# Six one-by-one releases of the q, k and v loads in a slot of selective attention, and fewer loads at the start

## The chip, the cores and the metric

One core of a Trainium2 chip runs the whole program. The metric is the device time of one execution in microseconds; the median of several executions counts, and less is better. The engines named below are PE (matmuls; its weight loads are listed as PEld), ACT (exponentials and copies), DVE (vector work), POOL (masks and indirect DMAs) and SP (which issues most DMAs). Each engine takes its instructions in the order in which the program gives them, and engines wait for each other through semaphores.

## The reference

The kernel computes a causal attention with a decaying bias for 8 batches of 8 heads, 576 tokens and head size 64, and then a mixture of eight experts over the tokens, in float32. Cut to what is computed:

```python
scores = scale * np.matmul(q, k.transpose(0, 1, 3, 2))
cum = np.cumsum(np.maximum(s, 0.0), axis=-1)
bias = -(cum[:, :, :, None] - cum[:, :, None, :])
scores = np.where(causal, -1000000000.0, scores + np.minimum(bias, 0.0))
attn = np.exp(scores - np.max(scores, axis=-1, keepdims=True))
attn = attn / (np.sum(attn, axis=-1, keepdims=True) + 1e-09)
x = np.matmul(attn, v)             # then (B,H,S,D) -> (B, S, H*D)
...
logits = x @ w_gate
local_gate = sigmoid(x @ w_local)
# token by token: keep the previous token's expert where local_gate >= 0.5, else argmax(logits)
h = np.maximum(x[b, s] @ w1[e], 0.0)
out[b, s] = softmax(logits[b, s])[e] * (h @ w2[e])
```

## The kernel before

The attention works on 32 pairs of heads (`NPAIR`), pair n being batch n // 4 and two neighbouring heads, which lie on the lower and upper 64 partitions. The main loop (L1002) runs over 16 slots m of two pairs each, 2m and 2m + 1. The program order is that of the Python code; no scheduler moves anything.

A slot has these parts, in this order:

- Scores (`scores`, L893): for each of the two pairs, four units u = 0 to 3 (`UNITS`). A unit is a handful of matmuls of keys by queries into one tile of the pool `ps_s` (three buffers of two PSUM banks), one exponential on ACT into the tile `e{u}` in SBUF (L905), and one or two causal masks on POOL (L890). A slot so has eight units and eight exponentials; `e` tiles have two buffers, one for each pair.
- The places 0 and 1, one after each pair's scores (`at`, L1016): planned work of the router, from slot 4 on. A product (`lp`) or a ranking (`pos`) takes one more `ps_s` buffer at place 1 of every second slot; from slot 6 on POOL stores tokens into a DRAM table with indirect DMAs (scatters, L349), up to five in a slot.
- Values (`values`, L924): for each pair, 200 matmuls a slot in all, in two pieces (query blocks 0 to 5, then 6 to 8), each into `po` in PSUM. Each piece is read out by DVE, a reciprocal into `recs` (L941) and a product (L942).
- Places 3, 4 and 5, and between them weighing (`weigh`, L876): v of a later pair, times the key weights, into one of four `vg` tiles; ACT writes one column (L881), DVE the rest (L884). `WEIGHED` says which pairs are weighed at the end of which slot: 2 and 3 in slot 0, 4 to 7 in slot 1, 8 and 9 in slot 2, and so on.

The inputs come through SP's DMA queue: q and k of a pair 288 KB each into `p_in` (four buffers each for q and k), v of a pair 320 KB into `p_v` (six buffers, `NVA`). At the start q, k of pairs 0 to 3 and v of pairs 0 to 5 are issued without a wait. Later loads are held back so that they do not start at once: before the DMA, ACT copies one element of something that is only ready at the wanted time into the tile to be loaded ("behind"), and the DMA has to wait for that copy. In every slot

- after unit 1 of the second pair, `load_v` of pair 2m + 6 is held behind that unit's exponential (L1014), and v of pair 2m + 7 follows at once, without a copy of its own;
- after the second value piece of the first pair is in `po`, and before DVE reads it out, `load_qk(n + NV)` holds k of pair 2m + 4 behind an element of `po` in PSUM (L1021), and q of that pair and k and q of pair 2m + 5 follow at once.

So a slot has two bursts, one of two transfers of v and one of four of k and q. After the attention the experts run: PE multiplies gathered tokens by w1 and w2 of each expert until the end.

Of the kernel before, what the change touches and what calls it, by code (L numbers as in the profile page):

```python
# [9 lines left out]
F32 = mybir.dt.float32  # L10
# [7 lines left out]
P = 128  # L18
B, H, S, DH = 8, 8, 576, 64
# [3 lines left out]
HP = H // 2  # L23
NPAIR = B * HP
# [11 lines left out]
NJ = S // DH  # L36
NJA = 6
# [8 lines left out]
NV = 4  # L46
NVA = 6
# [2 lines left out]
          ((5, 5), (0, 0, 1, 1, 3, 4, 5, 5)))  # L50
BX = 3
FIRST = ((0, P, 0, 3 * P), (P, S, 3 * P, S))
CAP = N + DH
ROWS = E * CAP + 2 * P
EMPTY = 1 << 20
# [60 lines left out]
class Router:  # L116
# [8 lines left out]
    def constants(self):  # L125
# [8 lines left out]
        self.base0 = self.t("base0", [P, E])  # L134
        nc.gpsimd.tensor_scalar(self.base0, self.eidx, float(CAP), 0.0, Alu.mult, Alu.add)
        self.base = self.t("base", [P, E])
# [18 lines left out]
    def constants2(self):  # L155
# [31 lines left out]
        for i in range(2 * DOUBLE // P):  # L187
            r = 2 * E * CAP + i * P
            nc.sync.dma_start(self.halves[r : r + P], self.pad)
# [190 lines left out]
    def assign(self, name, n, start, k, size):  # L380
# [11 lines left out]
        step = self.s(name + "step", [P, E])  # L392
        v.tensor_scalar(step, n, -float(size), float(CAP), Alu.mult, Alu.add)
        if start is not None:
# [6 lines left out]
        if start is not None:  # L401
            v.tensor_scalar(of[:, 1], r, start[:, 0:1], float(E * CAP), Alu.add, Alu.min)
        else:
            v.tensor_scalar(of[:, 1], r, float(E * CAP), None, Alu.min)
        used = self.s(name + "used", [P, E])
# [72 lines left out]
class Experts:  # L478
# [47 lines left out]
    def load(self, l, layer=None, part=None, behind=None):  # L526

        if l not in self.owner:
            return
        u = self.owner[l]  # L530
        if not part:
            self.e = self.piece(u, self.units[u][2].index(l), 0)
        parts = 1 if part is None else 4
        for i, src in enumerate((self.w1, self.w2)):
            if layer is not None and layer != i:
                continue
            ws = self.ws.setdefault(l, [None, None])
            if not part:
                pool = getattr(self, self.place(l))
                ws[i] = pool.tile([P, FK, D] if i else [P, DK, F], F32, name=f"w{i + 1}b")  # L540
                if behind is not None:
                    self.nc.scalar.copy(ws[i][0:1, 0, 0:1], behind)
            n = ws[i].shape[1] // parts
            c = slice((part or 0) * n, (part or 0) * n + n)
            self.nc.sync.dma_start(ws[i][:, c].rearrange("p c f -> p (c f)"),
                                   src[bass.ds(self.e, 1), :, c].rearrange("o p c f -> (o p) (c f)"))
# [219 lines left out]
def attention(ctx, tc, q, k, v, s, wx, ident, recs, wend, router, experts):  # L766
    nc = tc.nc
# [3 lines left out]
    def pool(name, bufs, **kw):  # L771
        return ctx.enter_context(tc.tile_pool(name=name, bufs=bufs, **kw))

    once = pool("once", 1)
    p_in = pool("p_in", 4)
# [11 lines left out]
    ins, vs, es, xs, xts = {}, {}, {}, {}, {}  # L787
    heads = [slice(DH * h, DH * h + DH) for h in range(2)]

    def load_qk(n, behind=None):  # L790

        if n >= NPAIR:
            return
        b, hp = divmod(n, HP)
        ins[n] = qb, kb = p_in.tile([P, S], F32, name="qb"), p_in.tile([P, S], F32, name="kb")
        if behind is not None:
            nc.scalar.copy(kb[0:1, 0:1], behind)
        for k0, k1, q0, q1 in FIRST if n == 0 else ((0, S, 0, S),):
            nc.sync.dma_start(kb[:, k0:k1], k[b][:, hp, k0:k1])  # L799
            nc.sync.dma_start(qb[:, q0:q1], q[b][:, hp, q0:q1])  # L800

    def load_v(n, behind=None):
        if n >= NPAIR:
            return
        b, hp = divmod(n, HP)
        va = vs[n] = p_v.tile([P, NB, 2, DH], F32, name="va")
        if behind is not None:
            nc.scalar.copy(va[0:1, 0, 0, 0:1], behind)
        nc.sync.dma_start(va.rearrange("p c h d -> p (c h d)"), v[b, hp].rearrange("p c h d -> p (c h d)"))
# [14 lines left out]
    load_qk(2)  # L824
    load_v(2)
    load_qk(3)
    for n in range(3, NVA):
        load_v(n)
    router.projection(wx)
    wk = once.tile([P, NPAIR, G1 + NB, 2], F32, name="wk")  # L830
    nc.gpsimd.memset(wk[:TL, :, G1 + NF], 0.0)
# [18 lines left out]
    def key_exps():  # L850
        nc.scalar.activation(w1, cum[:, : G1 * P], Act.Exp, bias=ref[:, 0:1])
        nc.scalar.activation(w2, cum, Act.Exp, bias=ref[:, 1:2])
# [40 lines left out]
    def scores(n, u):  # L893
        if n >= NPAIR:
            return
        qb, kb = ins[n]
        if u == 0:
            es[n] = [p_e.tile([P, 2, w], F32, name=f"e{i}") for i, w in enumerate(WIDTH)]
        e = es[n][u]
        ps = banks("ps")[:, :, : WIDTH[u]]  # L900
        for c, a, z, at in UNITS[u]:
            key = min(c * P, S - P)
            for h, d in enumerate(heads):
                mm(ps[:, h, at : at + z - a], lhsT=kb[d, key : key + P], rhs=qb[d, a:z], start=True, stop=True)  # L904
        nc.scalar.activation(e, ps, Act.Exp, scale=scale)  # L905
        for c, a, z, at in UNITS[u]:
            m = min(P, z - a)
            if a < c * P + P:
                masked(e[:, :, at : at + m], [[0, 2], [1, m]], P - m)

    def weights_of(n, c, j, h):
        for u, unit in enumerate(UNITS):
            for c1, a, z, at in unit:
                if c1 == c and a <= j * DH < z:
                    return es[n][u][:, h, at + j * DH - a : at + j * DH - a + DH]

    def x_tile(b):

        if b == 2:
            return p_x0.tile([P, NJ, 2, XW], F32, name="xb0")  # L920
        w = experts.w_first.tile([P, FK, D] if b else [P, DK, F], F32, name=f"w{b + 1}b")
        return w.rearrange("p c f -> p (c f)")[:, : NJ * 2 * XW].rearrange("p (j g f) -> p j g f", j=NJ, g=2)

    def values(n, j0, j1):  # L924
        b, hp = divmod(n, HP)
        if b not in xs:
            xs[b] = x_tile(b) if b < BX else p_x.tile([P, NJ, 2, XW], F32, name="xb")
        xb = xs[b]
        po = ps_o.tile([P, j1 - j0, VW], F32, name=f"po{j0}")
        for j in range(j0, j1):  # L930
            last = j // 2 if j < NJ - 1 else NF
            for c in range(last + 1):
                for h, d in enumerate(heads):
                    mm(po[d, j - j0, :], lhsT=weights_of(n, c, j, h),  # L934
                       rhs=vgs[n % NV][:, c if j < 2 * G1 else G1 + c, h, :],
                       start=(c == 0), stop=(c == last))

        def evacuate():
            m = j1 - j0
            rec = recs[:, n, j0:j1, :]  # L940
            nc.vector.reciprocal(rec, po[:, :, VW - 2 : VW])  # L941
            nc.vector.tensor_tensor(xb[:, j0:j1, :, 32 * hp : 32 * hp + 32], po[:, :, :DH].rearrange("p j (g i) -> p j g i", g=2),  # L942
                                    rec[:, :, 0].unsqueeze(2).unsqueeze(3).to_broadcast([P, m, 2, 32]), op=Alu.mult)

        return evacuate, po[0:1, 0, 0:1]

    def turn(n):

# [6 lines left out]
    def turns(pair):  # L955
        for n in pair:
            turn(n)
# [9 lines left out]
    for g in range(NG - 1):  # L967
        m = HP * GB // 2 * (g + 1)
# [9 lines left out]
        for c in range(NC):  # L978
# [3 lines left out]
            i, p = places[c]  # L982
# [3 lines left out]
    m = NPAIR // 2  # L986
# [11 lines left out]
    def at(slot, place):  # L998
        for f in todo.pop((slot, place), ()):
            f()  # L1000

    for m in range(NPAIR // 2):  # L1002
        pair = 2 * m, 2 * m + 1
        for n in pair:
            for u in range(len(UNITS)):
                if (n, u) == (0, 2):
                    key_exps()
                scores(n, u)
                if (n, u) == (0, 3):
                    key_weights()  # L1010
                    weigh(0)
                    weigh(1)
                if (n % 2, u) == (1, 1):
                    load_v(n - 1 + NVA, es[n][u][0:1, 0, 0:1])  # L1014
                    load_v(n + NVA)
            at(m, n - 2 * m)  # L1016
        for n in pair:
            values(n, 0, NJA)[0]()
            evacuate, done = values(n, NJA, NJ)
            if n % 2 == 0:  # L1020
                load_qk(n + NV, done)  # L1021
                load_qk(n + 1 + NV)
            evacuate()
            at(m, 3 + n - 2 * m)
        last = m % HP == HP - 1
        if last:
            turns(pair)
        for n in range(WEIGHED[m - 1] + 1 if m else 2, WEIGHED[m] + 1):
            weigh(n)
        if not last:  # L1030
            turns(pair)
        at(m, 5)
# [575 lines left out]
```

## Time and profile before

| | us |
|---|---|
| median of 3 runs | 729.42 (729.3 to 730.54) |
| the profiled execution | 748.85 |
| its span, first to last instruction | 747.1 |
| first score matmul | 4.84 |
| first expert matmul, after the attention | 221.6 |
| PE, 768 score matmuls (L904), busy | 94.7 |
| PE, 3200 value matmuls (L934), busy | 105.2 |
| ACT, 128 exponentials (L905), busy | 97.0 |
| POOL, 160 masks (L890), busy | 67.2 |

The profile is of one execution with the profiler on; its span is some 18 us above the median of the runs without it.[...] An entry such as "PEld ps <- ACT e" says that a weight load for the score tile `ps` stood still until ACT was done with `e`, which is read from semaphores. "issue" is time in which an engine stood still and nothing that the profile shows held it.

The start of the chain, and the loads as SP issues them (start, length, engine and line, tile):

```profile
0.81 0.39 SPq L799 DMA_DIRECT2D kb<-in_k_dram  x1
...
8.88 1.93 SPq L809 DMA_DIRECT2D va<-in_v_dram  x3
11.20 0.33 SPq L194 DMA_DIRECT2D wx<-in_wx_dram  x1
12.76 0.89 SPq L809 DMA_DIRECT2D va<-in_v_dram  x2
16.13 0.33 SPq L799 DMA_DIRECT2D kb<-in_k_dram  x1
16.51 0.45 SPq L800 DMA_DIRECT2D qb<-in_q_dram  x1
17.05 0.38 SPq L799 DMA_DIRECT2D kb<-in_k_dram  x1
17.48 0.42 SPq L800 DMA_DIRECT2D qb<-in_q_dram  x1
```

The three v at 8.88 are the last of the start, the two at 12.76 are the held ones of slot 0, and the four from 16.13 on are its held k and q.

### The profile page before, as it was taken

Reading aid. Unit: us, or ns where it says so; the run is one execution under the profiler, and the core shown is the slowest. Engines: PE = TensorE matmul, PEld = TensorE weight load, DVE = VectorE, ACT = ScalarE, POOL = GpSimd, SP = SyncE. Lnnn points to the kernel's source line nnn. Section 1 sums busy time; section 2 is a strip of 40 time slices with the busy share of each in tenths; the row PEclk is TensorE's granted clock in tenths of the full one; section 3 lists DMA queues with packets and bytes.
Section 4 is the critical chain, followed back from the end, with each engine's and each line's share of the span. In section 5 each row is a group of like instructions: output and inputs, shape, how many; then the busy total and the mean of one; then the engine's idle time right before and its main releaser. Section 6 shows DMA issues by size and latency. Waiting matters only on the chain.

```text
span 747.1 us, 16231 instructions
## 1 busy us (share of the span) xinstructions
PE 729.2 (98%) x6537; PEld 504.9 (68%) x6537; DVE 257.7 (34%) x714; ACT 166.0 (22%) x355; POOL 206.7 (28%) x453
## 2 busy tenths in 40 slices
PE   8999999999998999999999999999999999999996
PEld 7888878878876567567567365637644676673675
DVE  4656668677756383101100411041132001104110
ACT  4645454354331011011011010201010111110111
POOL 3543367577574245350100011010101001000100
PEclk9999999999998999999999999999999999999999
DMA  8464455665629996598555979996999965976700
GB/s 303 145 189 149 152 191 165 201 199 172 188 81 382 341 396 218 208 424 240 203 190 169 375 258 396 342 382 237 425 334 390 423 215 214 307 268 239 269 15 32
DMA packets 57205, 187.28 MB, mean 251 GB/s; under 512 B 11837, under 2 KB 32061, under 8 KB 49568
## 3 DMA queue, kind: packets, MB, share of 16 engines
q1 hardware_dynamic: 50224, 165.91, 62.3%
q0 software_dynamic: 6800, 20.09, 7.0%
q8 instruction: 53, 0.87, 0.5%
q14 instruction: 32, 0.26, 0.1%
q10 hardware_dynamic: 96, 0.15, 0.1%
HBM read 165.50 MB, written 20.75 MB: 249 GB/s over the span
## 4 chain that ended last, share of the span: by engine, by line
PE 95%; issue 2%; POOL 1%; DVE 1%; DMA 1%; ACT 0%; SPq 0%; POOLq 0%; ACTq 0%
PE yp L637 34%; PE hp L608 31%; PE po L934 13%; PE ps L904 11%; PE hp L599 4%; PE lp L217 2%; DMA qb<-in_q_dram 1%; POOL table L349 0%; ACT e L905 0%; PE pos L301 0%; POOL e L890 0%; PE pos L302 0%; DVE xb L942 0%; SPq L799 0%; POOL out_dram L641 0%
## 5 line engine op out<-in xcount | busy, mean ns | idle before, releaser
L637 PE MATMUL yp<-w2b,hT 128*128 128x512 f32 (+4 forms) x768 | 258.4, 584 | 0.0
L608 PE MATMUL hp<-xT,w1b 128*128 128x256 f32 (+2 forms) x1216 | 232.0, 352 | 0.0
L608 PEld LDWEIGHTS hp<-xT,w1b 128*128 128x128 f32 x1216 | 207.7, 192 | 30.0 <-issue 7.8
L637 PEld LDWEIGHTS yp<-w2b,hT 128*128 128x128 f32 (+3 forms) x768 | 109.9, 167 | 138.4 <-issue 136.1
L641 POOL DMA_INDIRECT out_dram<-y,gi x37 | 36.4, 984 | 412.3 <-DVE y L639 380.0
L610 ACT ACTIVATE hT<-hp 128x256 f32<-128x256 f32 (+2 forms) x152 | 53.6, 353 | 430.4 <-PE hp L608 417.2
L639 DVE TENSOR_SCALAR y<-yp,gi 128x512 f32<-128x512 f32 (+2 forms) x38 | 27.8, 731 | 299.8 <-PE yp L637 293.4
L934 PE MATMUL po<-vg,e 128*64 128x66 f32 x3200 | 105.2, 223 | 6.9 <-issue 5.6
L934 PEld LDWEIGHTS po<-vg,e 128*64 128x64 f32 x3200 | 98.7, 138 | 13.1 <-issue 10.5
L905 ACT ACTIVATE e<-ps 128x768 f32<-128x768 f32 (+1 forms) x128 | 97.0, 837 | 46.5 <-PE ps L904 45.8
L904 PE MATMUL ps<-qb,kb 64*128 64x192 f32 (+4 forms) x768 | 94.7, 398 | 0.6 <-ACT e L905 0.3
L904 PEld LDWEIGHTS ps<-qb,kb 64*128 64x128 f32 x768 | 64.7, 186 | 29.6 <-ACT e L905 14.9
L890 POOL TENSOR_SCALAR_AFFINE_SELECT e<-e 128x256 f32<-128x256 f32 (+1 forms) x160 | 67.2, 444 | 50.3 <-ACT e L905 49.3
L349 POOL DMA_INDIRECT table<-xb,idx x54 | 54.5, 1009 | 19.6 <-issue 16.8
L619 DVE STREAM_TRANSPOSE hT<-hs 32x256 f32<-32x256 f32 x64 | 27.9, 436 | 78.9 <-ACT hs L601 78.1
L884 DVE TENSOR_TENSOR vg<-va,wk 128x256 f32<-128x256 f32 x64 | 41.5, 714 | 0.0
L941 DVE RECIPROCAL recs<-po 128x12 f32<-128x12 f32 x64 | 13.5, 211 | 64.0 <-PE po L934 45.2
L599 PE MATMUL hp<-w1b,xT 128*32 128x512 f32 (+1 forms) x224 | 28.3, 594 | 0.0
L578 DVE STREAM_TRANSPOSE xT<-xq 128x1024 f32<-128x1024 f32 (+1 forms) x23 | 23.6, 1028 | 11.8 <-DMA xq<-table 11.7
L942 DVE TENSOR_TENSOR xb<-po,recs 128x384 f32<-128x384 f32 (+1 forms) x48 | 22.0, 458 | 2.2 <-POOL xb L325 0.6
L599 PEld LDWEIGHTS hp<-w1b,xT 128*32 128x32 f32 (+1 forms) x224 | 8.1, 114 | 17.8 <-issue 17.8
L953 DVE STREAM_TRANSPOSE xt<-xb 128x576 f32<-128x576 f32 x24 | 17.1, 751 | 0.0
(254 smaller groups left out, 202.6 us busy)
## 6 DMA issues: line engine op xcount, KB each, us to landing
w2b<-in_w_dram SPq DMA_DIRECT2D x30, 2048.0 KB
w1b<-in_w_dram SPq DMA_DIRECT2D x29, 2048.0 KB
va<-in_v_dram SPq DMA_DIRECT2D x32, 320.0 KB
kb<-in_k_dram SPq DMA_DIRECT2D x31, 288.0 KB
qb<-in_q_dram SPq DMA_DIRECT2D x31, 288.0 KB
xq<-table SPq DMA_DIRECT2D x56, 130.0 KB
w1b<-in_w_dram SPq DMA_DIRECT2D x4, 512.0 KB
xq<-table SPq DMA_DIRECT2D x20, 65.0 KB
```

The lines of the kernel that those rows point to most:

```text
L349: put = self.nc.gpsimd.indirect_dma_start(out=self.halves, in_=src, element_offset=0, in_offset=None, out_offset=bass.IndirectOffsetOnAxis ...
L599: mm(ps[d, :], lhsT=xT[:, k, d], rhs=self.ws[l][0][:, k, c * 512 : c * 512 + 512], start=(k == 0), stop=(k == DK - 1))
L608: mm(ps[:, :w], lhsT=self.ws[ls[0]][0][:, k, c * P : c * P + P], rhs=xT[:, k, :w], start=(k == 0), stop=(k == DK - 1))
L610: nc.scalar.activation(self.hT[u][:, c, :w], ps[:, :w], Act.Relu)
L619: self.nc.vector.transpose(hT[32 * a : 32 * a + 32, :, 32 * r : 32 * r + 32], hs[32 * r : 32 * r + 32].rearrange("p (c i) -> p c i", i=P)[ ...
L637: mm(ps[d, :], lhsT=hT[:, k, n * P + d.start : n * P + d.stop], rhs=self.ws[l][1][:, k, f : f + w], start=(k == 0), stop=(k == FK - 1))
L641: put = nc.gpsimd.indirect_dma_start(out=self.out[:, :], out_offset=bass.IndirectOffsetOnAxis(ap=gi.bitcast(I32)[:m, n, 0:1], axis=0), in_ ...
L884: nc.vector.tensor_tensor(vg[:, to].rearrange("p c h e -> p (c h) e")[:, :, :DH], va[:, :c].rearrange("p c h e -> p (c h) e"), wk[:, n, to ...
L890: nc.gpsimd.affine_select(out=ap, in_=ap, compare_op=Alu.is_ge, fill=0.0, base=base, pattern=n, channel_multiplier=-1)
L904: mm(ps[:, h, at : at + z - a], lhsT=kb[d, key : key + P], rhs=qb[d, a:z], start=True, stop=True)
L905: nc.scalar.activation(e, ps, Act.Exp, scale=scale)
L934: mm(po[d, j - j0, :], lhsT=weights_of(n, c, j, h), rhs=vgs[n % NV][:, c if j < 2 * G1 else G1 + c, h, :], start=(c == 0), stop=(c == last))
```

## The change

Every load after the start is held by a copy of its own. `parts_of(m)` lists what slot m has to load: v of pairs 2m + 4 and 2m + 5 (in slot 0 none, in slot 1 v of pairs 4 to 7), then k and q of pair 2m + 4 and k and q of pair 2m + 5. `let_go(place, behind)` is called after each score unit (place `e{u}{n % 2}`: unit u of the first or second pair) and after each read-out value piece (place `x{i}{n % 2}`), and where the place is among the slot's points it issues the next part behind that element: an element of the unit's `e` tile, in a column that POOL does not mask, or of `recs`, which DVE writes. In slots 2 to 13 the points are e00 and e20 (v), e01 (k), e21 (q), x00 (k) and x10 (q); slots 14 and 15 have nothing to load. At the start v of pairs 4 and 5 is no longer loaded, and slot 0 no longer loads v of pairs 6 and 7. The k copy no longer reads `po`.

```diff
+POINTS = {0: ("x00", "x10", "x01", "x11"), 1: ("e00", "e10", "e20", "e30", "e01", "e21", "x00", "x10"),
+          2: ("e00", "e20", "e01", "e21", "x00", "x10")}
...
-    for n in range(3, NVA):
-        load_v(n)
+    load_v(3)
...
-        return evacuate, po[0:1, 0, 0:1]
+        return evacuate
...
+    def qk_part(n, what):
+        def load(behind):
+            b, hp = divmod(n, HP)
+            to = p_in.tile([P, S], F32, name=what + "b")
+            ins.setdefault(n, [None, None])["qk".index(what)] = to
+            nc.scalar.copy(to[0:1, 0:1], behind)
+            nc.sync.dma_start(to, (q, k)["qk".index(what)][b][:, hp])
+        return load
+
+    def v_part(n):
+        return lambda behind: load_v(n, behind)
+
+    def parts_of(m):
+
+        v_of = {0: (), 1: range(NV, NV + 4)}.get(m, range(2 * m + NV, 2 * m + NV + 2))
+        return [v_part(n) for n in v_of if n < NPAIR] + [
+            qk_part(n, x) for n in (2 * m + NV, 2 * m + 1 + NV) if n < NPAIR for x in "kq"]
+
+    parts, points = [], {}
+
+    def let_go(place, behind):
+
+        if parts and place in points:
+            parts.pop(0)(behind)
+
     for m in range(NPAIR // 2):
         pair = 2 * m, 2 * m + 1
+        parts = parts_of(m)
+        points = POINTS.get(m, POINTS[2])
         for n in pair:
             for u in range(len(UNITS)):
...
-                if (n % 2, u) == (1, 1):
-                    load_v(n - 1 + NVA, es[n][u][0:1, 0, 0:1])
-                    load_v(n + NVA)
+                let_go(f"e{u}{n % 2}", es[n][u][0:1, 0, P : P + 1])
             at(m, n - 2 * m)
         for n in pair:
-            values(n, 0, NJA)[0]()
-            evacuate, done = values(n, NJA, NJ)
-            if n % 2 == 0:
-                load_qk(n + NV, done)
-                load_qk(n + 1 + NV)
-            evacuate()
+            for i, (j0, j1) in enumerate(((0, NJA), (NJA, NJ))):
+                values(n, j0, j1)()
+                let_go(f"x{i}{n % 2}", recs[0:1, n, j0, 0:1])
             at(m, 3 + n - 2 * m)
+        assert not parts
```

## The prediction

> **What bounds the kernel now.** I read the engine totals first, then the chain of waits, then PE's waits, and last the ScalarE (ACT) and weight-load (PEld) timelines of single slots, because the change touches only the attention stage (0 to 221.6 us, where the first expert matmul starts in the chain).
>
> ```profile
> PE 729.2 (98%) x6537; PEld 504.9 (68%) x6537; DVE 257.7 (34%) x714; ACT 166.0 (22%) x355; POOL 206.7 (28%) x453
> ...
> PE 95%; issue 2%; POOL 1%; DVE 1%; DMA 1%; ACT 0%; SPq 0%; POOLq 0%; ACTq 0%
> ```
>
> From PE's list of waits (total, times, longest):
>
> ```profile
> PEld ps L904 <- ACT e L905: 14.9, 42, 0.6
> ```
>
> TensorE is busy nearly always and the chain is PE; loads of q, k and v do not appear in it after the first 6 us. ACT looks idle (22%), but the last line says that weight loads of the score matmuls waited 42 times for an exponential. So I looked at how close ACT runs behind PE inside a slot. In slot 3 the scores run from 43.57 to 49.33 us, then 200 value matmuls take 5.98 us. Three windows of the score part, slots 3, 12 and 13 (columns: length, PE busy, PEld busy, clock, DMA share, GB/s):
>
> ```profile
> 43.57:49.33 5.76, 5.76 (x48) 4.05 (x48) 1.00 0.35 113
> 162.84:168.98 6.14, 6.14 (x48) 4.07 (x48) 1.00 0.51 196
> 178.15:184.25 6.10, 6.03 (x48) 4.05 (x48) 1.00 0.68 243
> ```
>
> The same 48 matmuls took 5.76 us in slot 3 and 6.14 in slot 12. The ACT and PEld timelines of slot 12 tell why:
>
> ```profile
> 163.86 0.81 ACT L905 ACTIVATE e<-ps 128x768 f32<-128x768 f32 x1 [0.70 <-issue]
> 164.89 3.79 ACT L905 ACTIVATE e<-ps 128x768 f32<-128x768 f32 x5 [0.21 <-PE ps L904]
> ```
>
> ```profile
> 166.62 1.00 PEld L904 LDWEIGHTS ps<-qb,kb 64*128 64x128 f32 x12 [0.57 <-ACT e L905]
> 168.02 0.89 PEld L904 LDWEIGHTS ps<-qb,kb 64*128 64x128 f32 x8 [0.40 <-ACT e L905]
> ```
>
> The second exponential began 164.89 - 163.86 = 1.03 us after the first; in slot 3 that step is 0.71 (45.30 - 44.59 below). ACT was 0.32 us late once, early in the slot, and the score part grew by 6.14 - 5.76 = 0.38. So in the score part ACT has no slack: score tiles rotate through three buffers (`ps_s`), unit u+3 cannot start before exponential u has been read, and one unit costs ACT as much as PE (5.76/8 = 0.72 us).
>
> [...]
>
> **The change, part by part.** *Copies on ACT.* A load is held back by a one-element ACT copy into its tile. Before there are 13 for v (L808) and 14 for k (L797), 27. After, every held load has its own: 4 in slot 0, 8 in slot 1, 6 in each of slots 2 to 13, 84 in all. What counts is where they stand. Before, the one copy among a slot's eight exponentials follows the sixth:
>
> ```profile
> 44.59 1.51 ACT L905 ACTIVATE e<-ps 128x768 f32<-128x768 f32 x2 [0.69 <-PE ps L904]
> 45.30 1.61 ACT L905 ACTIVATE e<-ps 128x768 f32<-128x768 f32 x2
> 48.19 0.84 ACT L905 ACTIVATE e<-ps 128x768 f32<-128x768 f32 x1
> 49.06 0.19 ACT L808 COPY va<-e 1x1 f32<-1x1 f32 x1
> 49.16 0.90 ACT L905 ACTIVATE e<-ps 128x896 f32<-128x896 f32 x1
> ```
>
> The copy reads the tile that the exponential just wrote, so it waits for its end (49.03), and the next starts at 49.16: 0.97 us from start to start where 0.69 to 0.71 is the rule. One such copy costs ACT 0.27 us, more than its own 0.19. After the sixth exponential that is free, because the slot's last unit (the eighth) waits only for the fifth.
>
> After the change slots 2 to 13 have copies behind exponentials 1, 3, 5 and 7 (places e00, e20, e01, e21). Two stand before the fifth. ACT is then 2 x 0.27 = 0.54 us late at the fifth, and the last score unit is late by as much, less a slack I take as 0.01 (slot 12 turned 0.32 into 0.38, so none): 12 slots x 0.53 = 6.4 us. In slot 1 copies follow each of the first four exponentials: 4 x 0.27 = 1.1 us. In slots 4, 6, 8, 10 and 12 a router product (`lp` or `pos`) takes the next score buffer, which waits for exponential 6, now 0.81 late while PE is 0.53 late; before it had about 0.1 to spare: 0.15 x 5 = 0.75. Together 8.2 us on PE.
>
> The copies at x00 and x10 wait for a DVE reciprocal during the value matmuls; queued behind them on ACT are only the weight-column copies (L881) and the next slot's exponentials, due at least 1 us after the slot starts (44.59 against 43.57). Nothing. The eighth exponential ends some 0.9 us later (49.96 + 0.78 before), its masks on POOL by about 52.4; PE, 0.53 late itself, wants them about 0.7 us into the second pair's values at 49.86 + 2.99 + 0.7 = 53.5. Covered; without that cover up to 0.9 us in a slot.
>
> *Removed.* The k copy no longer reads `po` in PSUM; the reciprocal behind it began with it at the end of the matmuls anyway: nothing. The copy after exponential 6 hid already: nothing.
>
> *Loads.* v 4 and 5 leave the start, v 6 and 7 leave slot 0, and all four come in the score part of slot 1, 7 us or more before they are weighed at its end[...]. SP has the same issues at about 0.4 us each. Cost nothing; without cover the weighing of slot 1 would be late, at most 1 us.
>
> *Relief.* The value blocks of the 16 slots, from first matmul to what follows, exceed 5.98 us by 15.1 us in sum: pauses of PE that the profile calls issue. Two fall where only loads run: in slot 0 and in slot 2, the first beside the initial loads (from the chain of waits; then PE and PEld rows of slot 15):
>
> ```profile
> 17.31 0.80 issue
> ...
> 42.17 0.08 issue
> ```
>
> ```profile
> 216.69 1.00 PE L934 MATMUL po<-vg,e 128*64 128x66 f32 x17
> 217.31 0.27 PEld L934 LDWEIGHTS po<-vg,e 128*64 128x64 f32 x6 [0.22 <-issue]
> 218.07 0.40 PE L934 MATMUL po<-vg,e 128*64 128x66 f32 x6 [0.37 <-issue]
> 218.84 0.29 PE L934 MATMUL po<-vg,e 128*64 128x66 f32 x3 [0.36 <-issue]
> ```
>
> The first two are worth 1.0 and 0.3 us of block time (7.01 and 6.28 against 5.98). I take half, 0.6. The rest come with the scatters from slot 7 on: the last four lines, in slot 15, lie where no q, k or v is loaded at all, 1 us after a scatter's start (215.98). From nothing to 5.3 us of pauses stand near a load burst; I take none of those. POOL's masks were waited for 1.2 us in all (PEld po behind POOL e); a later PE finds them done: 0.6 back.
>
> Sum: 8.2 - 0.6 - 0.6 = +7.0 us on the profiled execution's 748.85 us (span 747.1 and 1.75 around it). That stands 19.4 us above the median of 729.42, and part of the pauses may belong to profiling. The ACT steps are durations of instructions, so I carry them over whole: 729.4 + 7.0 = 736.4.
>
> **Rivals.** *A, faster: the spread cures the pauses.* [...]all 5.3 us near bursts go (slots 0, 2, 7, 8, 9, 11, 12), and 1.2 us of mask waits. [...]Against: slots 3 to 6 have the same bursts and blocks of 5.98; slot 13's pauses (187.4 to 189.2) come before its burst (189.5 on), and slot 15 has pauses and no burst. It decides from the point where the relief exceeds the copies' cost, which then must be about half of mine (one copy of two felt, 4.1): 729.4 - 6.5 + 4.1 = 727.0; with the copies free, 722.9. Chance 0.21. *B, no change:* ACT catches up because the copies turn out shorter than 0.27 or the three buffers hide them; the slot 12 window speaks against. 729.4, chance 0.06. *C, worse than mine:* the late last exponential delays POOL's masks in the slots with scatters, and a copy also waits on a scatter-stalled ACT: 0.9 us a slot, 12 x 0.9 + 1.5 = 12.3, 741.7. Slots 7 to 13 have POOL busy 8 to 11 of their 13 to 15 us; but there the masks wait for scatters, not ACT. Chance 0.08. My own case: 0.65.
>
> **How the numbers follow.** A measurement of this kernel can tell 0.2% (1.5 us) from no change. My case spans 733 (copies at 0.19 instead of 0.27: 5.8, with 2.2 of relief) to 739 (no relief, nothing absorbed, a little of C). Slower is 0.65 + 0.08 = 0.73, same 0.06, faster 0.21. The range holding 8 in 10 leaves out C's far end and A with free copies: 727.5 to 739.5.
>
> **What would show it.** Right: score parts of slots 2 to 13 near 6.3 us and of slot 1 near 6.9 instead of 5.76; PEld's wait for ACT e well above 14.9; steps between exponentials of about 0.97 behind a copy, at the first and third. Relief: the slot 0 value block near 6 instead of 7.01. Wrong: score parts still at 5.76 (then a copy costs ACT less than here), or value blocks of slots 7 to 12 near 5.98 (then bursts made the pauses, A).

## The result and the profile after

| | before | change |
|---|---|---|
| median of 6 runs, us | 729.61 (729.3 to 730.54) | 734.39 (734.04 to 735.09) |
| ratio, with its 95% interval | | 1.0063 (1.0052 to 1.0075) |
| the profiled execution, us | 748.85 | 734.15 |
| its span, us | 747.1 | 732.4 |

The change is 4.8 us slower (3.8 to 5.5 by the interval). The two profiled executions say the opposite, 747.1 against 732.4, and must not be subtracted. The change's was an execution like its unprofiled ones (734.15 beside 734.39), so profiling adds nothing here. Before's was another kind: it has 15.15 us of pauses inside its value blocks, and the page of the change has 1.01. The later profiles of before have them too, and where it was measured later, on three chips, its medians are 746.35 to 746.51, and 747.6 in the first experiment below. (Which chip the first measurement ran on is not on record.) A stage without those pauses can be compared between the pages; a total cannot.

The busy times, the chain and the costliest groups of the change's page:

```profile
PE 722.9 (99%) x6537; PEld 498.2 (68%) x6537; DVE 257.8 (35%) x714; ACT 176.5 (24%) x412; POOL 205.4 (28%) x453
...
PE 97%; ACT 1%; DMA 1%; issue 0%; SPq 0%; POOL 0%; POOLq 0%; DVE 0%; ACTq 0%
...
L905 PE MATMUL ps<-qb,kb 64*128 64x192 f32 (+4 forms) x768 | 100.3, 405 | 0.6 <-ACT e L906 0.3
L935 PE MATMUL po<-vg,e 128*64 128x66 f32 x3200 | 97.2, 223 | 0.6 <-issue 0.6
```

The busy time of the score matmuls grew from 94.7 to 100.3, by 5.6 us. It has waits in it: in slot 3 the same 48 matmuls read 6.18 us busy of 6.18, and 5.76 of 5.76 before. The value matmuls fell from 105.2 to 97.2, and "issue" fell from 2% of the chain to 0: these are the pauses, and the first two experiments below show that they go with the executions rather than with the change. ACT's 10.5 us more look harmless, 24% of the span; the list of PE's waits shows who pays:

```profile
PEld ps L905 <- ACT e L906: 23.1, 61, 0.7
```

It was 14.9 us in 42 waits. The windows of the score part of slots 1, 3, 12 and one without held loads, slot 14 (columns as in the prediction):

```profile
18.95:25.55 6.60, 6.47 (x48) 3.95 (x48) 1.00 0.80 240
43.71:49.89 6.18, 6.18 (x48) 4.00 (x48) 1.00 0.34 112
160.21:166.40 6.19, 6.19 (x48) 4.00 (x48) 1.00 0.82 252
186.93:192.69 5.76, 5.76 (x48) 4.05 (x48) 1.00 0.87 285
```

Slot 3 took 5.76 us before and 6.18 now, slot 1 takes 6.60, and in slot 14, where no copy stands, the part is 5.76 still. (Slot 15 has no copy either and takes 6.03, 0.27 more than before; ACT stands still for 0.17 us behind its second exponential there, for no reason that the profile shows.) The ACT timeline of slot 3 shows how:

```profile
44.73 0.81 ACT L906 ACTIVATE e<-ps 128x768 f32<-128x768 f32 x1 [0.69 <-PE ps L905]
45.57 0.19 ACT L810 COPY va<-e 1x1 f32<-1x1 f32 x1
45.67 1.59 ACT L906 ACTIVATE e<-ps 128x768 f32<-128x768 f32 x2
47.29 0.19 ACT L810 COPY va<-e 1x1 f32<-1x1 f32 x1
47.39 1.48 ACT L906 ACTIVATE e<-ps 128x768 f32<-128x768 f32 x2
```

The second exponential begins 45.67 - 44.73 = 0.94 us after the first, where slot 3 of before has 0.71. The first ends at 45.54, and only then, at 45.57, does the copy begin; in slot 3 of before, with no copy there, the second began at 45.30, ahead of the first's end at 45.40 (44.59 + 0.81). It happens again behind the third, before the fifth has been computed.

### The profile page after: what moved, and what is told of

Same layout as the page of the kernel before. It is cut to its first block, busy times and chain, and to the rows that moved or that the text cites. A ratio compares the mean times of both kernels' runs of the same rounds, so it can differ in the third digit from the quotient of the medians.

```text
span 732.4 us, 16397 instructions
## 1 busy us (share of the span) xinstructions
PE 722.9 (99%) x6537; PEld 498.2 (68%) x6537; DVE 257.8 (35%) x714; ACT 176.5 (24%) x412; POOL 205.4 (28%) x453
## 4 chain that ended last, share of the span: by engine, by line
PE 97%; ACT 1%; DMA 1%; issue 0%; SPq 0%; POOL 0%; POOLq 0%; DVE 0%; ACTq 0%
PE yp L639 35%; PE hp L610 31%; PE po L935 13%; PE ps L905 13%; PE hp L601 4%; PE lp L219 1%; DMA qb<-in_q_dram 1%; ACT e L906 0%; PE pos L303 0%; PE pos L304 0%; SPq L801 0%; POOL out_dram L643 0%; ACT xb L853 0%; POOLq L101 0%; ACT xb L852 0%
## 5 line engine op out<-in xcount | busy, mean ns | idle before, releaser
L906 ACT ACTIVATE e<-ps 128x768 f32<-128x768 f32 (+1 forms) x128 | 100.0, 824 | 39.8 <-PE ps L905 39.6
L905 PE MATMUL ps<-qb,kb 64*128 64x192 f32 (+4 forms) x768 | 100.3, 405 | 0.6 <-ACT e L906 0.3
L935 PE MATMUL po<-vg,e 128*64 128x66 f32 x3200 | 97.2, 223 | 0.6 <-issue 0.6
L935 PEld LDWEIGHTS po<-vg,e 128*64 128x64 f32 x3200 | 94.8, 138 | 2.7 <-issue 1.3
L905 PEld LDWEIGHTS ps<-qb,kb 64*128 64x128 f32 x768 | 64.3, 186 | 35.6 <-ACT e L906 23.1
```

Of the source, the lines that this page charges most:

```text
L935: mm(po[d, j - j0, :], lhsT=weights_of(n, c, j, h), rhs=vgs[n % NV][:, c if j < 2 * G1 else G1 + c, h, :], start=(c == 0), stop=(c == last))
```

## The experiments

All ran where before takes about 746.4 us, so each is told as a ratio to before, measured beside it on the same chip. The pauses are summed over the value blocks of all 16 slots in the profile (pause: what a block has above 5.98 us), the score parts over slots 1 to 15.

**Whose are the pauses: the kernel before again, unchanged.**

> The kernel before, once more, to see whether the pauses of PE in its first profile (15.1 us in the value blocks) belong to the kernel. If they belong to that one execution: span near 728, score parts 5.76 us, value blocks 5.98 in nearly all slots, and at most 2 us of pauses, in slot 0 and 2. If they belong to the kernel: span near 747 again with pauses from slot 7 on, and then the spread loads did cure them and something costs 15 us more than thought.

Measured: 747.6 us, ratio 1.0003 (0.999 to 1.0017). The pauses are back, 14.05 us in sum, mainly in slots 7 to 13 and 15 as in the first page, but hardly in slot 0 (6.07 us in place of 7.01). The score parts sum to 87.39. So the pauses come back with the longer time. That the executions of 729.6 us had none is likely but not shown, since none of them was profiled. The block of slot 0, on which the prediction built part of its relief, varies: 7.01, 6.07, 6.46, 6.82 and 6.90 us in the five profiles that have before's loads at the start.

**The change again.** It is the same kernel; only where it runs differs.

> The changed kernel, once more, on the chip that the other runs of this call share; in the call before, the kernel before took 746.5 us and showed 14 us of pauses in its value blocks, where it had taken 729.6. If the pauses come of the bursts, which the change spreads, they go: value blocks at 5.98, and on a chip where before takes 746 the change is faster, 746 + 6 - 5 to 14, so 738 to 747. If they come of that chip and the scatters, they stay, and the change is slower there as well, by 4 to 6 us. On a chip where before takes 729.6: 734.4 again.

Measured: 753.18 us, ratio 1.0089 (1.0071 to 1.0107), +6.6 us. Its pauses sum to 13.77, as before's (14.05, and 14.96 and 15.15 in its other two profiles). Two all-engine windows of slot 11, the scores and then the values (columns: length, then busy time of PE, PEld, DVE, ACT and POOL, clock, DMA share, GB/s):

```profile
152.07:158.27 6.20, 6.20 (x51) 4.01 (x49) 5.27 (x14) 5.08 (x10) 3.78 (x7) 1.00 0.45 134
158.27:166.58 8.31, 7.07 (x202) 6.52 (x201) 4.55 (x21) 2.31 (x8) 6.18 (x16) 1.00 0.77 214
```

And the same value block of the same kernel in the first measurement:

```profile
154.22:160.21 5.99, 5.99 (x203) 5.92 (x201) 3.21 (x17) 2.31 (x8) 5.49 (x14) 1.00 0.78 235
```

The loads are equally spread in both, ACT is busy 2.31 us in both, and one block takes 8.31 us and the other 5.99. Spreading the loads does not remove the pauses: rival A falls. The score parts sum to 92.97, +5.6 over before, and PE's waits for the exponentials are those of the first page:

```profile
PEld ps L905 <- ACT e L906: 23.2, 61, 0.7
```

The first expert matmul, which ends the attention, starts at 225.8 us, and in the three profiles of before at 221.3, 221.6 and 221.9. The attention so grew by 3.9 to 4.5 us, some 1.1 to 1.7 less than its score parts.

**The copies alone, two a slot.** Before, with two copies into a scratch element behind the first and third exponential, no load moved.

```diff
+                if n % 2 == 0 and u in (0, 2) and 2 <= m <= 13:
+                    nc.scalar.copy(probe, es[n][u][0:1, 0, P : P + 1])
```

> The kernel before with its bursts, and two more one-element copies on ACT, behind exponentials 1 and 3 of slots 2 to 13, into a tile that nobody reads. Theory: score parts of 6.19 us in these slots, 12 x 0.43 = 5.2 us more than 729.6, so 734.8. Rival (the loads' places cost): 729.6, score parts 5.76.

Measured: 751.2 us, ratio 1.0054 (1.0035 to 1.0072), +4.0 us. A score part and the ACT timeline of one slot:

```profile
43.82:50.01 6.19, 6.18 (x48) 4.01 (x48) 1.00 0.32 112
```

```profile
44.85 0.81 ACT L906 ACTIVATE e<-ps 128x768 f32<-128x768 f32 x1 [0.69 <-PE ps L905]
45.69 0.19 ACT L1015 COPY probe<-e 1x1 f32<-1x1 f32 x1
45.79 1.59 ACT L906 ACTIVATE e<-ps 128x768 f32<-128x768 f32 x2
```

The step is 0.94 and the score part 6.19, as in the change, with nothing held by these copies. The two copies before the fifth exponential make the longer score part of slots 2 to 13 by themselves, and the first expert matmul starts at 225.9 us, as late as in the change.

**One copy a slot.** The same with `u in (0,)`.

> The kernel before with one more copy on ACT, behind exponential 1 of slots 2 to 13. Theory: half of what two copies cost, score parts near 5.98, 12 x 0.21 = 2.5 us more than before. If ACT had slack for one copy: 5.76 and no change.

Measured: 747.79 us, ratio 1.0022 (1.0009 to 1.0035), +1.6 us.

```profile
31.24:37.21 5.97, 5.97 (x48) 3.99 (x48) 1.00 0.34 116
```

None, one and two copies give 5.76, 5.97 and 6.19: 0.21 us each, with no slack taken up first.

**What a copy's cost consists of.** The change, but each copy in the score part reads the previous exponential's tile, which is already done.

```diff
-                let_go(f"e{u}{n % 2}", es[n][u][0:1, 0, P : P + 1])
+                let_go(f"e{u}{n % 2}", (es[n][u - 1] if u else es[max(n - 1, 0)][3])[0:1, 0, P : P + 1])
```

> The changed kernel with each copy in the scores reading an element of the exponential before the one just issued, so the copy need not wait for the running one. If the cost of a copy is that wait[...]: a step of about 0.8 us instead of 0.94 between exponentials, score parts near 5.95, 734.4 - 12 x 0.24 - 0.4 = 731.1. If it is the copy itself: steps of 0.94 and 734.4 as before.

Measured: 750.08 us, ratio 1.0044 (1.0032 to 1.0056). Its ACT timeline and its window:

```profile
44.53 0.81 ACT L906 ACTIVATE e<-ps 128x768 f32<-128x768 f32 x1 [0.69 <-PE ps L905]
45.23 0.17 ACT L810 COPY va<-e 1x1 f32<-1x1 f32 x1
45.31 1.59 ACT L906 ACTIVATE e<-ps 128x768 f32<-128x768 f32 x2
```

```profile
43.50:49.40 5.90, 5.90 (x48) 4.01 (x48) 1.00 0.34 94
```

The copy now begins 0.70 us after the exponential's start, while it still runs, and the step is 0.78. Of the 0.23 us, 0.16 were waiting for the exponential just ahead, and 0.07 are what the copy costs without that wait. The score part loses 0.29 of its 0.43. The loads are still let go one by one as in the change; its score parts sum to 92.97, those of this run to 89.96, and the ratio falls from 1.0089 to 1.0044.

**Copies taken off ACT.** The change, with the copies inside the score part made by DVE; those behind value pieces stay on ACT.

```diff
-            nc.scalar.copy(va[0:1, 0, 0, 0:1], behind)
+            nc.vector.tensor_copy(va[0:1, 0, 0, 0:1], behind)
...
-            nc.scalar.copy(to[0:1, 0:1], behind)
+            (nc.scalar.copy if on_act[0] else nc.vector.tensor_copy)(to[0:1, 0:1], behind)
```

> The changed kernel with its six releases at the same places, but the copies in the scores done by DVE instead of ACT. Theory (only ACT's time ahead of the fifth exponential costs): score parts 5.76 us in slots 1 to 13, so 6.0 us below the change and within 1 us of before. Rival (the single transfers beside the scores cost): as slow as the change, 0.7 to 0.9% above before, with longer score or value blocks and no late exponentials.

Measured: 747.03 us, ratio 1.0007 (0.9994 to 1.002). The window and the ACT timeline of slot 3:

```profile
43.32:49.08 5.76, 5.76 (x48) 4.06 (x48) 1.00 0.47 158
```

```profile
44.34 5.95 ACT L906 ACTIVATE e<-ps 128x768 f32<-128x768 f32 x8 [0.63 <-PE ps L905]
```

Eight exponentials now run in one train, the score part is 5.76 again, and the loss is gone: the first expert matmul starts at 222.3 us, 3.5 earlier than in the change. The pauses stayed, 15.61 us in sum. But this version takes away the spread as well. DVE has other work queued ahead of the copies: in slot 5 it reaches all four of them between 75.59 and 75.75 us, and SP issues the loads back to back, from 75.73 on. In all slots from 5 to 13 its two v start 0.4 us apart, as in before; in the change they start 1.7 us apart. Slot 5 of this version, then of the change:

```profile
75.73 0.80 SPq L811 DMA_DIRECT2D va<-in_v_dram  x2
76.63 0.38 SPq L1009 DMA_DIRECT2D kb<-in_k_dram  x1
77.10 0.38 SPq L1009 DMA_DIRECT2D qb<-in_q_dram  x1
77.58 0.38 SPq L1009 DMA_DIRECT2D kb<-in_k_dram  x1
```

```profile
73.34 2.05 SPq L811 DMA_DIRECT2D va<-in_v_dram  x2
76.67 0.33 SPq L1009 DMA_DIRECT2D kb<-in_k_dram  x1
78.39 0.33 SPq L1009 DMA_DIRECT2D qb<-in_q_dram  x1
79.60 0.33 SPq L1009 DMA_DIRECT2D kb<-in_k_dram  x1
```

So this run shows that the rest of the change (the other start, the copies behind value pieces, the k copy that no longer reads `po`) costs nothing that can be told. It does not show what spread loads alone are worth. That ACT's copies cost the time rests on the three runs above; that the spread brings no gain rests on the change's own second measurement.

**The start alone.** Before, with v of pairs 4 and 5 out of the start, none loaded in slot 0, and v of pairs 4 to 9 loaded in slot 1 behind one copy.

```diff
-    for n in range(3, NVA):
-        load_v(n)
+    load_v(3)
...
-                    load_v(n - 1 + NVA, es[n][u][0:1, 0, 0:1])
-                    load_v(n + NVA)
+                    vs_now = () if m == 0 else range(NV, NVA + 4) if m == 1 else (n - 1 + NVA, n + NVA)
+                    for i, v_n in enumerate(vs_now):
+                        load_v(v_n, None if i else es[n][u][0:1, 0, 0:1])
```

> The kernel before with only the start of the change: v of pairs 4 and 5 not at the start and v of 6 and 7 not in slot 0, all four held once, behind the sixth exponential of slot 1. If the initial loads make the pause of slot 0: its value block 5.98 instead of 6.07 to 7.01, up to 1 us less than before. If not: no change.

Measured: 745.98 us, ratio 0.9999 (0.9985 to 1.0013); the value block of slot 0 takes 6.08 us, 6.07 to 7.01 in the unchanged kernel. Whatever the block gains, the time shows neither gain nor cost.

**Copies where they should be free.** The change, with its copies at other places: first none in the first pair's scores and the rest behind value pieces of both pairs, then all four in the second pair's scores.

```diff
-POINTS = {0: ("x00", "x10", "x01", "x11"), 1: ("e00", "e10", "e20", "e30", "e01", "e21", "x00", "x10"),
-          2: ("e00", "e20", "e01", "e21", "x00", "x10")}
+POINTS = {0: ("x00", "x10", "x01", "x11"), 1: ("e01", "e11", "e21", "e31", "x00", "x10", "x01", "x11"),
+          2: ("e01", "e21", "x00", "x10", "x01", "x11")}
```

> The changed kernel with the same six single releases, but no copy ahead of the fifth exponential of a slot (v at e01 and e21, k and q at the four x places; slot 1: v at e01, e11, e21, e31). Theory (copies ahead of the fifth exponential make ACT and so PE late): score parts back to 5.76 us in slots 1 to 13, 12 x 0.43 + 0.84 = 6.0 us less than 734.4, so 728.4. Rival (the single transfers spread over the slot cost, by traffic beside the scores or values): the transfers are as spread as before, so about 734.

Measured: 747.49 us, ratio 1.0007 (0.9991 to 1.0022). The score parts are 5.76 in slots 1 to 5, but 6.07 to 6.59 in slots 6, 7, 10, 12 and 13, and 6.75 in slot 14, where PE paused for 0.59 us. Slot 7's window and the ACT and DVE timelines ahead of it:

```profile
92.93:99.50 6.57, 6.15 (x48) 3.92 (x48) 1.00 0.36 115
```

```profile
93.82 0.19 ACT L1008 COPY kb<-recs 1x1 f32<-1x1 f32 x1 [3.27 <-DVE recs L942]
94.51 0.19 ACT L1008 COPY qb<-recs 1x1 f32<-1x1 f32 x1 [0.50 <-DVE recs L942]
94.61 0.31 ACT L882 COPY vg<-wk 128x14 f32<-128x14 f32 x2
```

```profile
90.64 0.30 DVE L312 TENSOR_TENSOR at<-pos,base 128x144 f32<-128x144 f32 x1
...
93.56 0.23 DVE L942 RECIPROCAL recs<-po 128x12 f32<-128x12 f32 x1
```

DVE does the router's chain from 90.64 on and reaches the reciprocal at 93.56. The copy on ACT waits 3.27 us for it, the second copy and two weight columns stand behind, and the first exponential of slot 7 starts at 94.82, 1.89 us after PE's first score matmul in place of some 1.0. Of the 5.6 us that the change had added to the score parts, only 2.3 were won back (their sum is 90.65): on ACT the copy's wait of 3.27 us was passed on to what was queued behind it, the second copy at 94.51, the weight columns at 94.61 and the exponential at 94.82. That the ratio is near 1 all the same owes something to the stage behind the attention, which took 18.2 us in this profile and 21.0 in before's on the same chip (the last section has more on it).

The other set of places was `2: ("e01", "e11", "e21", "e31", "x00", "x10")`, with slot 1 as above.

> The changed kernel with the six releases at e01, e11, e21, e31, x00, x10: no copy ahead of the fifth exponential, and none behind the read-out of the second pair, where the router's chain on DVE kept ACT waiting in the run with late points. Theory (copies ahead of the fifth exponential cost, the spread loads cost nothing): score parts 5.76 in all slots, 4.8 + 1.2 = 6 us below the change, so 1 us below before. Rival (spread loads cost): as slow as the change, 4.8 us above before.

Measured: 748.67 us, ratio 1.0036 (1.0019 to 1.0053), +2.7 us, though the score parts sum to 87.92, 0.5 above before. The loads are spread here, some 0.9 us apart. The same once more, and a profile of the kernel before on the same chip:

> The run with no copy ahead of the fifth exponential, again, since it came out 0.36% above before where 0.1% below was expected. If that was the noise of that chip: within 0.15% of before. If the later exponentials 6 to 8, up to 0.8 us behind, delay POOL's masks in the slots with scatters: 0.3% above before again, with value blocks of slots 7 to 13 about 2 us longer in sum than those of before.

> The kernel before, for its profile on the chip of this call. On a chip where it takes 746: 14 us of pauses in the value blocks, as before. On a chip where it takes 729.6: value blocks at 5.98 but for slot 0, score parts 5.76, span near 728.

Measured: 748.95 us, ratio 1.0037 (1.0021 to 1.0052); score sum 87.64 against 87.36 of the kernel before, pauses 16.08 against 14.96. The loss is real: it came twice. The two profiled executions differ by only 0.6 us (747.84 and 747.24), so their pages can't show where the 2.6 us between the medians lie; the two sums differ by 1.4. Slots 10 and 13 have longer value blocks in both profiles (7.81 and 8.82, then 7.57 and 10.60, against 6.98 to 7.02 and 7.81 to 7.90 before). That the later exponentials 6 to 8 delay the masks and so the values is a possibility, but in these two profiles PE's list of waits names no mask at all, and what is added in slot 13 are pauses put down to issue. Whether four later copies or the spread loads cost this time stays open.

No version came out faster than before.

## Why the prediction was right, step by step

- **The mechanism: right.** Copies on ACT ahead of the fifth exponential lengthened the score part (5.76, 5.97 and 6.19 us for none, one and two), so ACT had no slack there. That the three score buffers set this limit was the author's reading of the program; no run had another number of them. Copies without the spread reproduce it (1.0022 for one, 1.0054 for two), cheaper copies with the spread lower it (1.0044 for 1.0089), and with the score-part copies on DVE it is gone (1.0007).
- **A copy's cost: too large.** The prediction took 0.27 us, from the step behind the sixth exponential. Behind the first the steps are 0.94 against 0.71, 0.23 more, and two copies cost the score part 0.43 in place of 0.53: 12 x 0.43 = 5.2 us for 6.4. In slot 1 four copies cost 6.60 - 5.76 = 0.84 for 1.1. That ACT had no slack at all was right: 0, 1 and 2 copies go up by 0.21 and 0.22. The window of slot 12 was no proof of it, though: the line of the late exponential says that ACT stood still for 0.21 us waiting for PE's scores, so there PE was late and not ACT. The step was read wrongly and the conclusion held.
- **The extra 0.75 us for the router products in slots 4, 6, 8, 10 and 12: not there.** Slot 12's score part is 6.19, like slot 3's 6.18, and the product follows at once.
- **The sum on PE** was therefore 12 x 0.43 + 0.84 = 6.0 us, not 8.2; the busy time of the score matmuls rose by 5.6. Slots 12 and 13 of the kernel before were already at 6.1, and slot 15 added 0.27 that the prediction did not have.
- **Relief and absorption, 1.2 us: the size fits, the place only in part.** 5.6 us more in the score matmuls against 4.8 us more in time leaves 0.8 (0.1 to 1.8 by the interval of the ratio), and in the second measurement the attention absorbed 1.1 to 1.7. The relief did come where it was forecast: the value blocks of slots 0 and 2 are 5.98 us in both profiles of the change, where before has 6.07 to 7.01 and 6.28 to 6.34. But slot 3 has a pause in the change that the prediction did not have, with a block of 6.88 and then 7.56 us for 5.98 to 6.44 in before, which takes about as much again; why it pauses there wasn't found. PE's waits for masks, 0.9 to 1.4 us in before, are 0.7 in the change: 0.2 to 0.7 less, where 0.6 was forecast. No page of before without pauses exists, so the first measurement's 0.8 us can't be placed. The forecast of 736.4 was 2.0 us high, because its copies and products were 2.2 to 2.6 too dear.
- **Hidden costs of nothing: right.** The copies at x00 and x10, the missing k wait on PSUM and the later v loads leave no trace in the time: with the score-part copies on DVE the change costs nothing that can be told (1.0007). In the change's page a v of 320 KB took 3.4 us from issue to landing (the median), where the prediction left those of slot 1 at least 7.
- **Rival A** (spread cures the pauses) fell by the change's own second measurement, 13.77 us of pauses. Of the pauses that it counted on, those in slots 0 and 2 did go, but those from slot 7 on, which are most of them, did not. How a burst would make PE pause was not shown. **B** (hidden by three buffers) fell with 5.97 for one copy. **C** (late masks, 0.9 us a slot) is not seen in the change, where PE waited for masks 0.7 us in all; the open loss of the version with four late copies shows no such wait either.
- **Carrying ACT's durations from an execution of 748.85 us to those of 729.4 us: right.** The steps and score parts were the same in both kinds of execution (6.18 and 6.19, waits of 23.1 and 23.2), and so the difference carried over where the totals did not.

## What to carry to other kernels

An engine that is busy 22% of a kernel can still pace the bottleneck inside one stage, as ACT did here (6.19 us for 5.76): before putting even a one-element copy on it, compare its steps with the bottleneck's there, and see how far the buffers between them let it lag. Put such a hold behind the last unit that anyone waits for, and look at what is queued behind it, since its wait is theirs too (3.27 us of it, above). One copy in that place was free here (the score part of slot 3 took 5.76 us in before, and 5.76 with none on ACT); four were not (ratio 1.0036), for a reason that stays open. On an engine with room the hold can be cheap (1.0007 on DVE, which was busy 35% in the change), but it lets go only when that engine comes to it: here DVE turned single loads back into a burst (four copies between 75.59 and 75.75 us). And compare two pages block by block, after making sure that both executions are of the same kind; here the totals pointed the wrong way by 14.7 us.

## What the runs showed of the hardware

- One kernel has two levels: before took 729.6 us in the first measurement and 746.35 to 747.6 on three chips later, and its page of 748.85 belongs to the second. The change has a page at each level, with spans of 732.4 and 751.8 us. Of the 19.4 us between them, 12.9 lie ahead of the first expert matmul (at 212.93 and 225.79 us). They are the pauses in the value blocks, which come in the same slots each time (7 to 13 and 15, mostly those with scatters) and which the profile can give to no engine. The other 6.5 us lie in the stage that follows, up to the first product with w2:

```profile
212.93:228.60 15.67, 15.67 (x130) 13.59 (x130) 14.22 (x61) 2.97 (x9) 11.87 (x22) 1.00 0.85 322
225.79:247.94 22.15, 19.71 (x129) 16.11 (x130) 13.96 (x62) 3.20 (x9) 11.17 (x20) 0.85 0.87 352
```

- In that stage the granted clock was 1.00 at one level and 0.85 at the other (the column before the DMA share), and at the longer level four pauses of 2.4 us in sum stand in a router product. With two copies a slot the stage took 19.01 us, with four such pauses (2.3 us) but a clock of 1.00. By these figures the pauses and what goes with them cost some 3.3 us and the lower clock some 3.1 (an estimate: 19.01 - 15.67 and 22.15 - 19.01). What decides between the levels wasn't found.
- A one-element ACT copy of 0.19 us that read what ACT had just written delayed the next exponential by 0.23 us (0.94 against 0.71 from start to start); one of 0.17 us that read an older result, by 0.07 (0.78 against 0.71). On DVE the same copies, 0.14 us for one and 0.16 for two in a row in slot 3, took nothing that the time shows (ratio 1.0007).
